# Twelve units on half the tokens first, none of them stored, and the products of chunks 2 and 3 stepped between those of chunks 0 and 1

## The chip, the cores and the metric

The kernel runs on one core of a Trainium2 chip. The metric is the device time of the whole program in microseconds (us), from the first to the last instruction with what lies around them. Three runs of the kernel before gave a median of 1481.88 us.

## The reference

Three stages follow each other. `S` is 768 steps, `N` is 4 x 768 = 3072 tokens.

```
for t in range(S):                       # 4 batches, 8 heads, 48 x 48 state
    S_re, S_im = ar*S_re - ai*S_im + k v^T, ar*S_im + ai*S_re
    y[:, :, t] = q . S_re
x = y as (3072, 384)
out = sum over 4 experts of p_e * (relu(x @ w1[e]) @ w2[e])   # 1024 wide each
h = out @ w_in                           # 2048 wide
result = maximum(0.01*h, h) @ w_out
```

`a` is first scaled so that its magnitude is at most 0.999, and `p` is the expert probability divided by its sum.

## The kernel before

**Tiling.** The recurrence is cut into 24 chunks of 128 steps. For a chunk, `elementwise(c)` (17 steps, on VectorE, ScalarE and GpSimd) makes decayed and rotated queries and keys in the tile `ft`, and six DMAs (`by_head`, L251) rearrange it by head into `hd`. `products(c)` (9 steps) is TensorE work: transposes `pt` copied to `kt`, scores `sc` masked into `att`, the state update `pm` into `st`, the output `py` copied to `y`, and transposes `px` split into `xh` and `xl`, a high and a low part whose sum is the fp32 value. Four chunks fill a token group of 512.

**Units.** The first weight stage is 32 units of 128 hidden columns, the second 16. A unit of the first stage is loaded as `raw` (384 KB, L392), split into two parts by `split_unit` (ScalarE cast L408, GpSimd difference L409; once for the in-weights, part 0, and once for the out-weights, part 1), and used: `gemm_in` (L455) makes `ph`, VectorE and ScalarE turn it into `hp` (L460), `hh` (L472) and `hl` (L473), and `gemm_out` (L484 to L486) adds into three accumulators. Six parts are split early instead, with TensorE making the difference (`cast_early` L419, `rest_early` L429 to L431). A unit that was split is stored to `ws_scratch` (768 KB, L626), and later groups load it from there (L400).

**Order.** The program is recorded by hand, and each engine runs its instructions in the order of recording. `PLAN` is the order of the start: digits step `elementwise`, `p` and `q` step the products of chunks 0 and 1, `s` and `m` are `cast_early` and `rest_early`. The list `order` then names the units. In group 0, eight units run on tokens 0 to 255 (chunks 0 and 1), then the same eight on tokens 256 to 511 (chunks 2 and 3), and units 8 to 31 on all 512. For each entry, `gemm_in` stands two entries ahead of `gemm_out`, and between the halves of an entry `tick` takes up to three steps of `background()`: the rest of chunks 2 and 3, their products (`r`, `t`), and all later chunks at a pace set by a table. SyncE issues nearly all DMAs, in order, so a DMA that waits for its data holds up those behind it.

**Names.** "In block" and "out block" are the nine matmuls of one `gemm_in` or `gemm_out`; "in 5" is that of the entry 5. "Pair" is the two wide matmuls of one `rest_early`.

Of the kernel before, what the change touches and what calls it, by code (L numbers as in the profile page):

```python
# [19 lines left out]
P = 128  # L20
# [12 lines left out]
AR_MIN = 0.76  # L33
NHALF = 8
PLAN = (
    "0101001010101011" "01ss0000mm" "00sss11mm000" "1111ppsm23111qq"
    "23232n3pp23p2ppqq3q23qqpq23m"
)
MAXT = 3
KN = 3.0  # L40
PT = 32
TPOOL = 6
MARGIN = 2.0
LAG = 2
E2 = 20
RAWS = 4
# [5 lines left out]
NSTEPS = ESTEPS + len(PSTEPS)  # L52
WAIT = 4
AR_MAX = 1e4
# [7 lines left out]
def fused_kernel(  # L62
# [20 lines left out]
    with ExitStack() as fast:  # L83
# [58 lines left out]
        def load_chunk(c, part=None):  # L142
            if part in (None, 0):
                pool = p_el2 if c in (1, 3) else p_in
                t = pool.tile([P, 4, NG, P], F32, name="aaqk", bufs=2)
                vt = pool.tile([P, DM], F32, name="vt", bufs=2 if c in (1, 3) else 3)
                inputs[c] = (t, vt)
            t, vt = inputs[c]
            if part is None:
                SP.dma_start(t, attn[c])  # L150
            else:
                SP.dma_start(t[:, 2 * part : 2 * part + 2], attn[c][:, 2 * part : 2 * part + 2])
            if part in (None, 1):
                SP.dma_start(vt, v[c])
# [3 lines left out]
        def table(name):  # L158
            if tables[0] != name:
                A.preload_act_table_set(name)  # L160
                tables[0] = name

        def elementwise(c):
# [79 lines left out]
        def by_head(c):  # L243
# [4 lines left out]
            for ri in range(2):  # L248
                for i in range(NG):
                    row = ri * D + i * DG  # L250
                    (A if c < 2 and (i == ri or i == 2 - ri) else SP).dma_start(hd[row : row + DG], ft[:, ri, i])  # L251
            feats[c] = (ft, hd, vt)
# [5 lines left out]
        def products(c):  # L258
# [7 lines left out]
            for ri in range(2):  # L266
                pt = ps_a.tile([P, NG, P], F32, name="pt", tag="pa")
                for i in range(NG):
                    PE.transpose(pt[:, i], ft[:, ri, i, P : 2 * P], ident)  # L269
                A.copy(  # L270
                    kt[:, :, ri * D : (ri + 1) * D].rearrange("t h (r d) -> t r d h", d=DG),
# [28 lines left out]
            for h in range(H):  # L300
                PE.matmul(py[:, h], att[:, h], vt[:, h * D : (h + 1) * D], start=True, stop=first)  # L301
                if not first:
                    PE.matmul(py[:, h], hd[:, h, :P], old[:, h], start=False, stop=True)  # L303
                if h == 3:
                    yield
# [62 lines left out]
        second_stage = lambda g: [(g, u, whole) for u in range(NU1, NU)]  # L368
        order = [(0, u, half) for half in halves for u in range(NHALF)] + first_stage(0)[NHALF:]
        begins = [0]  # L370
# [10 lines left out]
        raws, wts, pbs, hs, x2 = {}, {}, {}, {}, {}  # L381
        seen = set()
        fresh = [u not in seen and not seen.add(u) and u < NU1 for _, u, _ in order]

# [51 lines left out]
        def load_pb(s):  # L436
            if s >= len(order) or order[s][1] >= NU1 or order[s][1] % 8 or order[s][2][0]:
                return
            g, e = order[s][0], order[s][1] // 8
            pb = p_h.tile([P, TG], F32, name="pb", bufs=2)  # L440
            SP.dma_start(pb, pn_d[e : e + 1, g * TG : (g + 1) * TG].to_broadcast([P, TG]))
# [34 lines left out]
        def gemm_out(s, acc):  # L476
            u, (t0, t1) = order[s][1:]
            first, last = u in (0, NU1) and t0 == 0, u in ends
            wt = wts.pop(s)[:, 1]
            hh, hl = hs.pop(s)  # L480
            for dc in range(NG):
                cols = slice(dc * P, (dc + 1) * P)
                out = acc[dc][:, t0:t1]
                PE.matmul(out, wt[:, 0, cols], hh, start=first, stop=False)  # L484
                PE.matmul(out, wt[:, 1, cols], hh, start=False, stop=False)  # L485
                PE.matmul(out, wt[:, 0, cols], hl, start=False, stop=last)  # L486


        def zipped(*gens):
            gens = list(gens)  # L490
            while gens:
                for x in list(gens):
                    if next(x, gens) is gens:
                        gens.remove(x)
                yield

        def run_all(*gens):
            gens = list(gens)
            while gens:
                gens = [x for x in gens if next(x, gens) is not gens]  # L500

        with tc.manual_schedule():
# [12 lines left out]
            steps.update(zip("pqrt", (products(c) for c in range(CPG))))  # L515
            early_halves = iter([(s, part) for s in range(6) for part in (0, 1)][: PLAN.count("s")])
            for x in PLAN + "m" * 8:
                if x in steps:
# [6 lines left out]
                elif x == "m":  # L525
                    rest_early()
            for s in (5, 6):
                load_unit(s)
            split_unit(3, 0)

            def background():
                for _ in range(2):
                    next(steps["2"])
                    yield
                for _ in zipped(steps["2"], steps["3"]):
                    yield
# [36 lines left out]

            first = 2 + max(0, ESTEPS + 1 - min(PLAN.count("2"), PLAN.count("3"))) + WAIT + E2 - PLAN.count("r") - PLAN.count("t")
            pace = [(0.0, 0), (KN, first)]
# [33 lines left out]
            for s in range(len(order)):  # L609
# [14 lines left out]
                split_h(s + 2, hp)  # L624
                if fresh[s]:
                    SP.dma_start(ws[u], wts[s].bitcast(F32))  # L626
# [216 lines left out]
```

## Time and profile before

| | us |
|---|---|
| median of three runs | 1481.88 |
| lowest, highest | 1481.4, 1482.5 |
| the profiled execution | 1478.36 |
| its span, first to last instruction | 1476.6 |
| TensorE busy (95% of the span) | 1402.4 |
| VectorE busy (59%) | 864.7 |
| ScalarE busy (38%) | 564.8 |
| GpSimd busy (18%) | 264.5 |

The page cuts the span into 40 slices of 37 us and gives each engine's busy share in tenths; a 9 is 90% or more. An engine whose row is all nines has no room there. The view of waits says for whom an engine stood idle, the timeline gives each instruction its start and duration, and the view by windows gives busy time and granted TensorE clock of any stretch. A clock of 1.00 is 2.4 GHz, 0.50 is 1.2 GHz.

### The profile page before, as it was taken

What the parts mean: (1) busy time and instruction counts of PE and PEld (TensorE: products, weight loads), DVE (VectorE), ACT (ScalarE), POOL (GpSimd) and SP (SyncE); (2) the same over time, 40 slices, a digit from 0 to 9 for tenths busy, and PEclk for the clock granted to TensorE, in tenths of its full rate; (3) what the DMA queues carried; (4) which work ended last, traced back from release to release, by engine and by line L of the source; (5) the groups of instructions that cost most, each with busy time, mean ns of one, the idle gap of its engine ahead of it and who ended that gap; (6) DMA issues with size and microseconds to landing.
All of it is one profiled execution on the core that took longest, in us unless ns stands there. A gap on an engine that the chain in (4) does not pass through costs nothing.

```text
span 1476.6 us, 18540 instructions
## 1 busy us (share of the span) xinstructions
PE 1402.4 (95%) x6978; PEld 1177.2 (80%) x6978; DVE 864.7 (59%) x1504; ACT 564.8 (38%) x961; POOL 264.5 (18%) x244
## 2 busy tenths in 40 slices
PE   3858999999999999999999999999999999999997
PEld 1858888888777888788888888888888888888886
DVE  7556887788988898785454554554443333333332
ACT  5424565444345434455234354233332111323232
POOL 2120565412223223221011110110110000100000
PEclk9569999999999999999999999999999999999999
DMA  7288789986788789588567477576465665556561
GB/s 192 43 207 301 212 255 298 331 291 208 273 301 290 250 305 319 153 303 245 153 234 222 151 242 216 188 222 199 154 199 172 231 207 196 190 188 208 190 212 65
DMA packets 91043, 325.49 MB, mean 220 GB/s; under 512 B 10464, under 2 KB 32064, under 8 KB 90944
## 3 DMA queue, kind: packets, MB, share of 16 engines
q1 hardware_dynamic: 87488, 318.71, 67.1%
q10 hardware_dynamic: 3456, 5.51, 1.3%
q8 instruction: 56, 0.92, 0.3%
q14 instruction: 43, 0.35, 0.1%
HBM read 262.72 MB, written 42.52 MB: 207 GB/s over the span
## 4 chain that ended last, share of the span: by engine, by line
PE 58%; DVE 2%; ACT 0%; issue 0%; DVEq 0%; ACTq 0%
PE ph L455 27%; PE acc L484 9%; PE acc L486 9%; PE acc L485 9%; PE sc L280 1%; PE py L301 1%; PE py L303 1%; PE pm L289 1%; PE pt L269 0%; DVE hl L473 0%; DVE hp L460 0%; PE px L311 0%; DVE d L349 0%; ACT hh L472 0%; DVE d L355 0%
## 5 line engine op out<-in xcount | busy, mean ns | idle before, releaser
L455 PE MATMUL ph<-xh,wt 128*128 128x512 f32 (+1 forms) x1200 | 397.9, 388 | 0.0
L484 PE MATMUL acc<-hh,wt 128*128 128x512 f32 (+1 forms) x888 | 350.8, 395 | 5.2 <-ACT o L604 5.1
L486 PE MATMUL acc<-hl,wt 128*128 128x512 f32 (+1 forms) x888 | 342.9, 386 | 4.5 <-DVE hl L473 4.5
L485 PE MATMUL acc<-hh,wt 128*128 128x512 f32 (+1 forms) x888 | 341.5, 385 | 0.0
L472 ACT CAST hh<-hp 128x512 fp32r<-128x512 f32 (+1 forms) x296 | 180.4, 610 | 418.2 <-DVE hp L460 326.5
L473 DVE TENSOR_TENSOR hl<-hp,hh 128x512 fp32r<-128x512 f32 (+1 forms) x296 | 213.4, 721 | 150.3 <-ACT hh L472 149.1
L455 PEld LDWEIGHTS ph<-xh,wt 128*128 128x128 f32 x1200 | 225.5, 190 | 42.4 <-ACT ge L121 0.3
L460 DVE SCALAR_TENSOR_TENSOR hp<-ph,pb 128x512 f32<-128x512 f32 (+1 forms) x200 | 133.0, 665 | 189.9 <-PE ph L455 188.6
L455 PE MATMUL ph<-xl,wt 128*128 128x512 f32 (+1 forms) x600 | 230.2, 384 | 0.0
L486 PEld LDWEIGHTS acc<-hl,wt 128*128 128x128 f32 x888 | 167.3, 188 | 40.0 <-DVE hl L473 6.0
L455 PE MATMUL ph<-x2h,wt 128*128 128x512 f32 x576 | 198.3, 398 | 0.0
L484 PEld LDWEIGHTS acc<-hh,wt 128*128 128x128 f32 x888 | 167.7, 189 | 36.5 <-ACT o L604 5.8
L485 PEld LDWEIGHTS acc<-hh,wt 128*128 128x128 f32 x888 | 168.0, 189 | 30.7
L463 DVE SCALAR_TENSOR_TENSOR hp<-hp 128x512 f32<-128x512 f32 x96 | 72.0, 750 | 185.0 <-ACT hp L462 184.9
L455 PEld LDWEIGHTS ph<-xl,wt 128*128 128x128 f32 x600 | 114.1, 190 | 20.3 <-DVE xl L320 0.2
L455 PEld LDWEIGHTS ph<-x2h,wt 128*128 128x128 f32 x576 | 108.7, 189 | 25.1
L462 ACT COPY hp<-ph 128x512 f32<-128x512 f32 x96 | 56.3, 586 | 178.5 <-PE ph L455 178.5
L455 PE MATMUL ph<-x2l,wt 128*128 128x512 f32 x288 | 114.5, 397 | 0.0
L409 POOL TENSOR_TENSOR wt<-raw,wt 128x384 fp32r<-128x384 f32 x58 | 65.0, 1142 | 62.4 <-ACT wt L408 62.3
L643 POOL TENSOR_TENSOR x2l<-o,x2h 128x512 fp32r<-128x512 f32 x18 | 25.2, 1424 | 256.4 <-ACT x2h L642 256.4
L301 PE MATMUL py<-vt,att 128*128 128x48 f32 x384 | 70.9, 280 | 0.1
L280 PEld LDWEIGHTS sc<-hd 96*128 96x128 f32 x384 | 54.2, 208 | 15.4 <-issue 7.9
(97 smaller groups left out, 1482.2 us busy)
## 6 DMA issues: line engine op xcount, KB each, us to landing
wt<-ws_scratch SPq DMA_DIRECT2D x264, 768.0 KB, 4.8
ws_scratch<-wt SPq DMA_DIRECT2D x32, 768.0 KB, 7.5
hd<-ft SPq DMA_DIRECT2D x138, 128.5 KB, 5.4
aaqk<-in_attn_dram SPq DMA_DIRECT2D x22, 768.0 KB, 8.9
raw<-in_w_dram SPq DMA_DIRECT2D x32, 384.0 KB, 4.5
r<-in_w_dram SPq DMA_DIRECT2D x32, 384.0 KB, 7.4
ws_scratch<-dw SPq DMA_DIRECT2D x32, 384.0 KB, 6.2
pb<-pn_scratch SPq DMA_DIRECT2D x24, 256.0 KB, 6.5
```

What stands on the lines that cost most here:

```text
L280: PE.matmul(sc[:, j], hd[:, h, P : 2 * P], hd[:, h, :P], start=True, stop=True)
L301: PE.matmul(py[:, h], att[:, h], vt[:, h * D : (h + 1) * D], start=True, stop=first)
L409: G.tensor_tensor(wt[:, 1], raw, wt[:, 0].bitcast(F32), ALU.subtract)
L455: PE.matmul(ph[:, : t1 - t0], wt[:, wi, cols], x[kc][:, t0:t1], start=n == 0, stop=n == 3 * NG - 1)
L460: V.scalar_tensor_tensor(hp, ph, 0.0, pbs[g, u // 8][:, t0:t1], ALU.max, ALU.mult)
L462: A.copy(hp, ph)
L463: V.scalar_tensor_tensor(hp, hp, 0.01, hp, ALU.mult, ALU.max)
L472: A.copy(hh, hp)
L473: V.tensor_tensor(hl, hp, hh.bitcast(F32), ALU.subtract)
L484: PE.matmul(out, wt[:, 0, cols], hh, start=first, stop=False)
L485: PE.matmul(out, wt[:, 1, cols], hh, start=False, stop=False)
L486: PE.matmul(out, wt[:, 0, cols], hl, start=False, stop=last)
```

## The change

The list `order` runs twelve units on tokens 0 to 255, then units 12 to 19 on all 512, and then alternates: the second half of unit 0, unit 20 whole, the second half of unit 1, unit 21 whole, and so on to unit 31. The first halves store nothing; the twelve second halves load `raw` again, split it again and store it, so the eight loads from `ws_scratch` in group 0 are gone and twelve loads of `raw` are new. Twelve parts instead of six are split early on TensorE. `PLAN` is rewritten, the products of chunk 1 get four additional 384-column matmuls (`warm`) whose result nobody reads, their `kt` copies go from ScalarE to VectorE, and three `hd` DMAs of chunk 1 go from ScalarE's queue to SyncE's. `LATER` orders the rest of the elementwise steps of chunks 2 and 3.

```
-NHALF = 8
+NHALF = 12
 PLAN = (
-    "0101001010101011" "01ss0000mm" "00sss11mm000" "1111ppsm23111qq"
-    "23232n3pp23p2ppqq3q23qqpq23m"
+    "0101001010101011" "01ss0000mm" "00sss11mm000" "1111ppsmsm23111L"
+    "23n22qqsmsm33ppsm22p3ppmsqqm3qsm2233qqpqm"
 )
+LATER = "23222232232223333333"
-KN = 3.0
+KN = 5.0
-WAIT = 4
+WAIT = 22
...
+        def warm(n):
+            out = ps_acc.tile([P, TG], F32, name="warm", tag="acc0")
+            for _ in range(n):
+                PE.matmul(
+                    out[:, : NG * P], ident, inputs[0][0][:, 0].rearrange("p g t -> p (g t)"),
+                    start=True, stop=True,
+                )
...
-                    (A if c < 2 and (i == ri or i == 2 - ri) else SP).dma_start(hd[row : row + DG], ft[:, ri, i])
+                    (A if c == 0 and (i == ri or i == 2 - ri) else SP).dma_start(hd[row : row + DG], ft[:, ri, i])
...
-                A.copy(
+                (V.tensor_copy if c == 1 else A.copy)(
...
+                if c == 1 and h % 2:
+                    warm(1)
...
-        order = [(0, u, half) for half in halves for u in range(NHALF)] + first_stage(0)[NHALF:]
+        order = [(0, u, halves[0]) for u in range(NHALF)] + first_stage(0)[NHALF : NU1 - NHALF]
+        for u in range(NHALF):
+            order += [(0, u, halves[1]), (0, NU1 - NHALF + u, whole)]
...
-        fresh = [u not in seen and not seen.add(u) and u < NU1 for _, u, _ in order]
+        fresh = [g == 0 and u < NU1 for g, u, _ in order]
...
+            parts = [(t0, t1)]
+            if (order[s][0], u) == (0, NHALF):
+                parts = list(halves)
...
             def background():
-                for _ in range(2):
-                    next(steps["2"])
-                    yield
-                for _ in zipped(steps["2"], steps["3"]):
+                for x in LATER:
+                    next(steps[x], None)
                     yield
...
-                if fresh[s]:
+                if fresh[s] and t1 == TG:
                     SP.dma_start(ws[u], wts[s].bitcast(F32))
```

What moves is shown at three places. The first is TensorE between the output of chunk 0 (`py`, L301, now L311) and the end of the products of chunk 1. Before:

```order
L301 MATMUL py<-vt,att 128x48 x8
L280 MATMUL sc<-hd 128x128 x8
L289 MATMUL pm<-vt,kt 96x48 x8
L301 MATMUL py<-vt,att 128x48
L303 MATMUL py<-st,hd 128x48
```

Now:

```order
L311 MATMUL py<-vt,att 128x48 x8
L442 MATMUL ph<-raw,ident 128x384
L443 MATMUL ph<-wt,minus 128x384
L290 MATMUL sc<-hd 128x128 x8
L442 MATMUL ph<-raw,ident 128x384
L443 MATMUL ph<-wt,minus 128x384
L299 MATMUL pm<-vt,kt 96x48 x8
L442 MATMUL ph<-raw,ident 128x384
L443 MATMUL ph<-wt,minus 128x384
L311 MATMUL py<-vt,att 128x48
L313 MATMUL py<-st,hd 128x48
```

Pairs of wide matmuls now stand between the narrow ones.

The second place is ScalarE around the copies `kt` of chunk 2 (`kt_657` before, `kt_833` now), with buffer numbers; `raw_509` and `raw_718` are each the newest unit whose part 0 is cast there (unit 7 before, unit 11 now). Before:

```order
L408 CAST wt_567<-raw_467 128x384
L472 CAST hh_643<-hp_637 128x256
L270 COPY kt_657<-pt_658 128x48x8
L270 COPY kt_657<-pt_663 128x48x8
L408 CAST wt_670<-raw_509 128x384
```

Now:

```order
L488 CAST hh_801<-hp_799 128x256
L421 CAST wt_816<-raw_718 128x384
L421 CAST wt_784<-raw_674 128x384
L280 COPY kt_833<-pt_834 128x48x8
L280 COPY kt_833<-pt_839 128x48x8
```

The cast of the newest unit moved from behind the two copies to ahead of them.

The third place is SyncE's queue from the `hd` pieces of chunk 2 on; `aaqk` and `vt` are the inputs of chunk 4. Before:

```order
L626 DMA ws_scratch<-wt 128x1536 x2
L251 DMA hd<-ft 16x8x257 x12
L150 DMA aaqk<-in_attn_dram 128x1536
L154 DMA vt<-in_v_dram 128x384
L626 DMA ws_scratch<-wt 128x1536
```

Now:

```order
L457 DMA pb_628<-pn_scratch 128x512
L261 DMA hd<-ft 16x8x257 x6
L405 DMA raw<-in_w_dram 128x768
L261 DMA hd<-ft 16x8x257 x6
L151 DMA aaqk<-in_attn_dram 128x1536
L155 DMA vt<-in_v_dram 128x384
L405 DMA raw<-in_w_dram 128x768 x7
```

The `raw` of unit 10 stands between the `hd` pieces of chunks 2 and 3, and those of units 11 to 17 behind chunk 3's and the inputs of chunk 4.

## Rows read from the trace of the kernel before

**Rows 1.** The page: its first line, and TensorE's busy tenths in 40 slices.

```profile
span 1476.6 us, 18540 instructions
...
PE   3858999999999999999999999999999999999997
```

**Rows 2.** Windows: stretch, length, busy time (instructions) by engine, clock, DMA share, GB/s.

```profile
36.00:66.00 30.00, 25.32 (x120) 24.19 (x121) 13.38 (x31) 11.04 (x21) 0.00 (x0) 0.50 0.25 43
...
123.00:170.00 47.00, 41.44 (x271) 37.07 (x269) 37.63 (x73) 27.56 (x51) 17.59 (x16) 0.96 0.71 213
...
222.00:259.00 37.00, 35.77 (x192) 29.90 (x191) 28.91 (x47) 22.07 (x39) 21.87 (x20) 1.00 0.95 302
259.00:296.00 37.00, 37.00 (x206) 31.68 (x206) 26.79 (x40) 18.29 (x33) 15.40 (x14) 1.00 0.97 331
```

**Rows 3.** TensorE's waits, 66 to 128 us: in total, times, longest.

```profile
PE pt L269 <- DVE ft L234: 9.4, 1, 9.4
PE sc L280 <- DMA hd<-ft: 5.4, 1, 5.4
```

**Rows 4.** TensorE's timeline, products of chunks 0 and 1: start, duration, what [idle before].

```profile
36.47 3.79 PE L280 MATMUL sc<-hd 96*128 96x128 f32 x16 [2.04 <-ACT kt L270]
...
44.47 2.79 PE L289 MATMUL pm<-vt,kt 128*96 128x48 f32 x16 [4.21 <-DVE att L281]
47.06 3.61 PE L301 MATMUL py<-vt,att 128*128 128x48 f32 x16
...
63.33 1.67 PE L311 MATMUL px<-ident,y 128*128 128x128 f32 x6
...
66.74 0.58 PE L455 MATMUL ph<-xh,wt 128*128 128x256 f32 x1
```

**Rows 5.** Windows: one microsecond after `py` of chunk 2 (columns as above).

```profile
107.00:108.00 1.00, 0.68 (x7) 0.55 (x5) 0.00 (x0) 0.29 (x1) 0.00 (x0) 0.82 1.04 430
```

**Rows 6.** TensorE's timeline at the full clock: a pair, an out block's start, products.

```profile
24.97 0.81 PE L429 MATMUL ph<-raw,ident 128*128 128x384 f32 x2
25.62 0.81 PE L430 MATMUL ph<-wt,minus 128*128 128x384 f32 x2
...
70.27 0.28 PE L484 MATMUL acc<-hh,wt 128*128 128x256 f32 x1
...
71.35 0.28 PE L455 MATMUL ph<-xh,wt 128*128 128x256 f32 x1
...
112.35 1.16 PE L280 MATMUL sc<-hd 96*128 96x128 f32 x8 [0.56 <-ACT kt L270]
...
115.32 1.48 PE L289 MATMUL pm<-vt,kt 128*96 128x48 f32 x16
...
122.01 0.55 PE L311 MATMUL px<-ident,y 128*128 128x128 f32 x3 [0.57 <-ACT y L307]
```

**Rows 7.** The chain that ended last: a whole unit's in block.

```profile
623.15 2.10 PE ph L455 x9
```

**Rows 8.** VectorE's timeline: chunk 2's wait at 39 us, `ft` of chunks 2 and 3.

```profile
39.03 0.56 DVE L185 TENSOR_TENSOR ta<-ta,tb 128x384 f32<-128x384 f32 x1 [5.33 <-ACT ta L121]
...
85.77 0.95 DVE L234 TENSOR_TENSOR ft<-cs,aaqk 128x768 f32<-128x768 f32 x1
...
87.78 2.62 DVE L234 TENSOR_TENSOR ft<-cs,aaqk 128x768 f32<-128x768 f32 x2
```

**Rows 9.** ScalarE's timeline: the table load ahead of chunk 2's elementwise work.

```profile
37.08 1.28 ACT L160 ACT_TABLE_LOAD   x1
```

**Rows 10.** SyncE's timeline: the `hd` pieces of chunks 2 and 3.

```profile
86.75 7.71 SPq L251 DMA_DIRECT2D hd<-ft  x12
```

**Rows 11.** Windows: transfers while `hd` pieces move, and while units' loads and stores do.

```profile
96.00:100.00 4.00, 4.00 (x22) 4.00 (x21) 1.20 (x2) 0.00 (x0) 0.00 (x0) 0.50 1.18 122
...
172.00:174.00 2.00, 2.00 (x12) 1.65 (x10) 1.97 (x5) 0.00 (x0) 0.00 (x0) 1.00 1.02 415
```

**Rows 12.** Groups by line, GpSimd, 150 to 262 us: count | busy, mean ns | idle before.

```profile
L409 POOL TENSOR_TENSOR wt<-raw,wt 128x384 fp32r<-128x384 f32 x43 | 48.8, 1158 | 26.0 <-ACT wt L408 25.9
```

More of the change, by code (lines that the diff above doesn't have):

```diff
@@ L44 @@
 LAG = 2
-E2 = 20
+E2 = 17
 RAWS = 4
@@ L145, in load_chunk @@
                 t = pool.tile([P, 4, NG, P], F32, name="aaqk", bufs=2)
-                vt = pool.tile([P, DM], F32, name="vt", bufs=2 if c in (1, 3) else 3)
+                vt = (p_el2 if c == 1 else p_in).tile([P, DM], F32, name="vt", bufs=1 if c == 1 else 3)
                 inputs[c] = (t, vt)
@@ L381, in fused_kernel @@
         raws, wts, pbs, hs, x2 = {}, {}, {}, {}, {}
-        seen = set()
-        fresh = [u not in seen and not seen.add(u) and u < NU1 for _, u, _ in order]
+        fresh = [g == 0 and u < NU1 for g, u, _ in order]
         def load_unit(s):
@@ L439, in load_pb @@
             g, e = order[s][0], order[s][1] // 8
-            pb = p_h.tile([P, TG], F32, name="pb", bufs=2)
+            if g == 0 and e * 8 < NHALF:
+                pb = pools["raw"].tile([P, TG], F32, name=f"pb{e}")
+            else:
+                pb = p_h.tile([P, TG], F32, name="pb", bufs=2)
             SP.dma_start(pb, pn_d[e : e + 1, g * TG : (g + 1) * TG].to_broadcast([P, TG]))
@@ L480, in gemm_out @@
             hh, hl = hs.pop(s)
+            parts = [(t0, t1)]
+            if (order[s][0], u) == (0, NHALF):
+                parts = list(halves)
             for dc in range(NG):
                 cols = slice(dc * P, (dc + 1) * P)
[L483 to L494, printed above, removed]
-                yield
[L497 to L500, printed above, removed]
+                for a0, a1 in parts:
+                    out = acc[dc][:, a0:a1]
+                    hhp, hlp = hh[:, a0 - t0 : a1 - t0], hl[:, a0 - t0 : a1 - t0]
+                    PE.matmul(out, wt[:, 0, cols], hhp, start=first, stop=False)
+                    PE.matmul(out, wt[:, 1, cols], hhp, start=False, stop=False)
+                    PE.matmul(out, wt[:, 0, cols], hlp, start=False, stop=last)
         with tc.manual_schedule():
@@ L515, in fused_kernel @@
             steps.update(zip("pqrt", (products(c) for c in range(CPG))))
-            early_halves = iter([(s, part) for s in range(6) for part in (0, 1)][: PLAN.count("s")])
-            for x in PLAN + "m" * 8:
+            early_halves = iter([(s, part) for s in range(7) for part in (0, 1)][: PLAN.count("s")])
+            for x in PLAN:
                 if x in steps:
@@ L526, in fused_kernel @@
                     rest_early()
-            for s in (5, 6):
-                load_unit(s)
-            split_unit(3, 0)
+                elif x == "L":
+                    load_unit(5)
+                    load_unit(6)
             def background():
-                for _ in range(2):
-                    next(steps["2"])
-                    yield
-                for _ in zipped(steps["2"], steps["3"]):
+                for x in LATER:
+                    next(steps[x], None)
                     yield
@@ L572, in fused_kernel @@
             dec = decoding()
-            first = 2 + max(0, ESTEPS + 1 - min(PLAN.count("2"), PLAN.count("3"))) + WAIT + E2 - PLAN.count("r") - PLAN.count("t")
+            first = len(LATER) + WAIT + E2
             pace = [(0.0, 0), (KN, first)]
```

## The prediction

> **What bounds the kernel now.** I read the slices of the page first: TensorE is at 90% or more from the fifth slice to the end [rows 1], so from about 150 us on the time is TensorE's own work, and only the first 150 us hold room. Then I read the waits and the windows of that part. Between 36 and 66 us TensorE is busy 25.3 of 30 us, but at a clock of 0.50 [rows 2]: the products of chunks 0 and 1 run at half speed. The first in block starts at 66.74 [rows 4]; I call that moment T0. After T0 TensorE stands 9.4 us for `ft` of chunk 2 and 5.4 us for its `hd` [rows 3]. The transposes `px` of chunk 3 end at 122.01 + 0.55 = 122.56 [rows 6], 55.8 us after T0. From 123 to 170 us only 47.0 - 41.4 = 5.6 us are idle [rows 2], and less later. So the change can gain in three ways: an earlier T0, more gemm work done before 122.56, and fewer waits after it.
>
> **The start, up to T0.** Six more pairs stand on TensorE, and four `warm` matmuls. At full clock a matmul of 384 columns takes 25.62 - 24.97 = 0.65 us [rows 6], a pair 1.3 us. The products at half clock and at full clock, from rows: a block of 8 `sc` 3.79 against about 2.1 us (half of it 1.16 with its tail), `pm` 2.79 against 1.48 [rows 4, 6], `py` of chunk 0 3.61 us [rows 4] against an estimated 1.8, `py` of chunk 1 twice that.
>
> What releases them moves too. The table load at 37.08 [rows 9] comes earlier, because ScalarE no longer issues three DMAs of chunk 1 nor copies its `kt`; two casts and a difference copy take some of that room. I put it at 33.5, and VectorE's wait of 5.33 us at 39.03 [rows 8] shrinks by 3.6 us. VectorE's `kt` copies then end at about 38.4, so `sc` of chunk 0 starts at about 38.6 instead of 36.47 [rows 4]; it has two more pairs ahead of it in any case. From there TensorE has no long wait that I can find, and I add at full clock: `sc` 2.1, pair 1.3, `pm` 1.5, `py` 1.8, pair 1.3, `sc` 2.1, pair 1.3, `pm` 1.5, pair 1.3, `py` 3.6 with four `warm` 2.6, which is 20.4 us, to 59.0. Of what follows, `px`, `xh` and `xl`, about 1.8 us are uncovered: T0 at 60.8, **5.9 us earlier**.
>
> The clock is the choice in this. Before, narrow matmuls alone did not raise it in 30 us, and behind `py` of chunk 2 it fell again at 107 (0.82 on the way to 0.50 [rows 5]); at 115.32 `pm` still ran fast behind `sc` [rows 6]. With pairs between the narrow blocks I take the full clock, since the row at 115 is the nearer one. If it falls for the second half, `sc`, `pm` and `py` of chunk 1 cost 1.7 + 1.3 + 3.3 = 6.3 us more.
>
> The Trainium skill, "TensorE: Matmul & The Clock Gate", section "Why this matters for your kernels", asks only that TensorE be kept busy without a pause to reach its high clock. By that page alone the pairs and `warm` would buy no clock and just cost their 6 x 1.3 + 2.6 = 10.4 us, against 3.6 from the earlier table load: T0 at 73.5, and the sum +7.4 instead of the -5.3 below. The 25.3 busy microseconds at 0.50 [rows 2] contradict it, so it gets no chance here.
>
> **T0 to the end of the products of chunk 3.** VectorE paces this. Before, `ft` of chunk 2 was ready at 85.77 + 0.95 = 86.72 and that of chunk 3 at 90.40 [rows 8]: 20.0 and 23.7 us after T0. In the new order six scans (2.7 us) are done ahead of T0, about two more `hp` and `hl` (1.8 us) stand between, and `ft` of chunk 2 goes ahead of the last steps of chunk 3. I get 17.5 and 23.5 us after T0. While VectorE works, TensorE gets through ten in and seven out blocks instead of five and three.
>
> Then comes what I think is the new bound. Twelve `hd` pieces took 7.7 us to issue [rows 10] and moved at 122 GB/s [rows 11]; six of them are 0.79 MB, 6.4 us. So chunk 3's move from 25.3 to 31.7 us after T0. Behind them on SyncE's queue stand the inputs of chunk 4 (0.98 MB) and `raw` of unit 11 (0.39 MB), at 415 GB/s [rows 11] another 3.3 us: it lands at about 36 us after T0. ScalarE casts unit 11 ahead of the `kt` copies of chunk 2, and `sc` needs the buffer that `kt` frees. So `sc` of chunk 2 starts at about 37.8 instead of 95.70 - 66.74 = 29.0 (its wait ended there). TensorE stands for about 9 us, and the clock falls. From there to the end of `px` of chunk 3 I count five blocks and two chunks' products, 20.9 us at full clock, 2.4 for the clock, 2.1 for the known short waits: 25.4. The stretch is 63.2 us instead of 55.8: **7.4 us longer**.
>
> In return more is done by then. Before, eight in and six out blocks had run; now it is twelve and ten. A half block is 71.35 - 70.27 = 1.08 us [rows 6], so 8 x 1.08 = **8.6 us less remain**.
>
> **What is added after.** Four more units are cut in two: each costs 4 x 1.08 - 2 x 2.10 [rows 7] = 0.12 us, and unit 12's out block is cut as well: 0.6, with the spread of these blocks **0.8 us**. In 12 now stands right behind `px` of chunk 3 and waits for `xh` and `xl`; before, an out block stood between: **1.0 us**. The other waits of 123 to 170 us I leave as large as they are: some of them came from halves that are gone, and GpSimd gets new work. That work is 18 more differences at 1.158 us [rows 12], 21 us, and ScalarE as many casts; GpSimd is busy 21.9 of 37 us there [rows 2], and at this load they hide. Were GpSimd full, they would cost up to 21 us.
>
> **Sum:** -5.9 + 7.4 - 8.6 + 0.8 + 1.0 = **-5.3 us**. The profiled execution took 1478.36 us, its span 1476.6, and the median is 1481.88. I put the difference on the median: **1476.6 us**. A difference below 0.2%, 3.0 us, can't be told from none.
>
> **The rivals.**
>
> *Transfers too slow in the alternation (slower).* A second half and a whole unit, 2.16 + 4.20 = 6.4 us of TensorE, now move two stores of 0.79 MB and two loads of 0.39 MB: 2.36 MB. Twelve such and three chunks at 1.77 MB are 33.6 MB against 76 + 3 x 8.6 = 102 us of TensorE. Needed are 330 GB/s. Before, 331 were sustained over 37 us at a share of 0.97 without a wait, but only 302 in the stretch ahead [rows 2]. At 302 it takes 111 us: 9 us more, 1485.6. It decides from below 330 GB/s on; four buffers of `raw` hold a load at most three entries ahead, so a late one stops ScalarE and then TensorE. Against it: single stretches reach 415 [rows 11], and with `hd` at its own pace I get 19 + 31.2 MB / 415 = 94 us.
>
> *The limit of the HBM.* If the weights moved at a steady 358 GB/s and `hd` as above, the transfers would take 19 + 87 = 106 us, 4 us over TensorE's 102: 1480.6. The Trainium skill, "DMA: Bandwidth & Descriptors", section "Where 436 GB/s comes from", states 358 as the limit of one core's share of the HBM. By that rule this change would be bound by it; the window at 415 speaks against it.
>
> *The clock falls in the products of chunk 1.* T0 at 67.1: -5.3 + 6.3 = +1.0, 1482.9. For it speaks the fall at 107, against it the row at 115.
>
> *Unit 11 lands early, or its cast doesn't block.* Then `sc` of chunk 2 starts when its `hd` lands and TensorE gets there, about 29 us after T0: 8.8 us less, 1467.8. For it: several DMAs are in flight at once, so `raw` may pass. Against it: the 122 GB/s lasted as long as `hd` moved, with a load of inputs already issued behind it.
>
> **How the numbers follow.** The forecast (1473 to 1479) gets 0.50, slow transfers 0.17, the limit of the HBM 0.05, the fallen clock 0.15, the early unit 11 0.13. Faster: 0.44 of the forecast, the early unit 0.13, and the lower edges of the limit and the clock 0.05, together 0.62. Same: 0.05 of the forecast, 0.08 of the clock, 0.02 of the limit, 0.03 of the slow transfers, 0.18. Slower: the other 0.20. The range goes from 1467 to 1486; both ends take in the rivals up to their own prices and leave about 2 in 10 outside.
>
> **What would show it.** Right: the first in block near 61 us; a clock of 1.00 from 37 us to it; `sc` of chunk 2 waiting some 9 us, with ScalarE waiting for `raw` of a weight cast just ahead of `kt`; `px` of chunk 3 ending near 124; TensorE without long waits after. Wrong: half clock in `py` of chunk 1; `sc` of chunk 2 released by `hd` instead; TensorE waiting for GpSimd or for weights between 160 and 270 us, with the transfers at a share near 1.

## The result, and the profile after

The changed kernel took **1496.3 us** (median of 4 runs, 1495.9 to 1498.7) against 1481.6 us (4 runs, 1480.8 to 1482.5): a ratio of 1.0107, 95% interval 1.0090 to 1.0124. It is slower by 14.7 us. The prediction was 1476.6 us with a range of 1467 to 1486, so sign and range are both wrong. The profiled execution of the changed kernel took 1495.9 us, close to its median; that of the kernel before took 1478.4, 3.2 us below its median. Some 3 us of any difference between these two traces are spread of the runs. Their spans differ by 17.6 us: 13.2 arise up to the emptying of the accumulators of group 0 (at 285.7 us before, at 298.9 now), and 4.4 behind it, where no cause was looked for. One of the twelve executions of the experiment e7 below took 2295.5 us at a granted clock of 0.58; without it the median of e7 is 1479.2 us instead of 1479.4.

The first line of the page and TensorE's busy tenths in 40 slices of 37 us, to be read against [rows 1]:

```profile
span 1494.2 us, 18843 instructions
...
PE   4869898899999999899999999999999999999997
```

The fifth to the eighth slice, 149 to 299 us, were all 9 before and are 9, 8, 8, 9 now. The windows of the changed kernel (stretch, length, busy time by engine, granted clock, DMA share, GB/s) cut the time at the first in block, at the end of the products of chunk 3, and where the accumulators of group 0 are emptied (299 us, before 286):

```profile
36.00:59.00 23.00, 21.85 (x144) 17.29 (x143) 15.32 (x31) 12.60 (x27) 2.08 (x2) 1.00 0.62 137
60.00:124.00 64.00, 47.88 (x344) 45.24 (x344) 33.25 (x61) 19.82 (x42) 18.47 (x17) 0.85 0.37 84
124.00:299.00 175.00, 152.38 (x884) 132.70 (x884) 133.51 (x211) 95.67 (x177) 95.69 (x84) 0.94 0.85 266
```

The same last stretch of the kernel before:

```profile
123.00:286.00 163.00, 155.12 (x884) 133.32 (x883) 129.24 (x214) 92.64 (x167) 80.54 (x72) 0.99 0.86 266
```

This pair of rows holds the result. Before, TensorE was idle for 163.0 - 155.1 = 7.9 us of that stretch, and the clock cost another 1.7 (in windows of half a microsecond, busy time times what the clock lacks to 1.00, added up). Now it is idle for 175.0 - 152.4 = 22.6 us, and the clock costs 8.0. That is 14.7 + 6.3 = 21 us more lost. The stretch should have become 7 us shorter and became 12 us longer; the work in it fell by the other 9. TensorE's waits there (in total, times, longest):

```profile
PE sc L290 <- DMA hd<-ft: 13.4, 4, 4.3
PE pt L279 <- DVE ft L244: 5.6, 1, 5.6
PE px L323 <- ACT y L319: 2.7, 2, 1.8
```

Each of chunks 4 to 7 waits at `sc` for its `hd`, and chunk 4 for its `ft`. Behind the longer stops the clock is low. The last `sc` stop, and the five microseconds that follow:

```profile
269.70 3.76 PE L290 MATMUL sc<-hd 96*128 96x128 f32 x16 [4.13 <-DMA hd<-ft]
```

```profile
270.00:275.00 5.00, 5.00 (x25) 5.00 (x25) 3.05 (x5) 1.78 (x4) 2.19 (x3) 0.50 1.01 419
```

So a stop of 4.1 us costs about 2.5 us more at half clock (5.0 x 0.50).

### The profile page after: what moved, and what is told of

Its sections match the earlier page's. It is cut to its first block, busy times and chain, and to the rows that moved or that the text cites. A ratio compares the mean times of both kernels' runs of the same rounds, so it can differ in the third digit from the quotient of the medians.

```text
span 1494.2 us, 18843 instructions
## 1 busy us (share of the span) xinstructions
PE 1410.0 (94%) x7091; PEld 1180.6 (79%) x7091; DVE 879.9 (59%) x1514; ACT 577.2 (39%) x993; POOL 289.3 (19%) x262
## 4 chain that ended last, share of the span: by engine, by line
PE 57%; issue 0%; ACT 0%; DVE 0%
PE ph L471 26%; PE acc L505 9%; PE acc L507 9%; PE acc L506 9%; PE sc L290 1%; PE py L311 1%; PE py L313 1%; PE pm L299 1%; PE pt L279 0%; PE px L323 0%; DVE hp L479 0%; ACT o L610 0%; ACT hh L488 0%; ACT hp L478 0%; ACT dw L369 0%
## 5 line engine op out<-in xcount | busy, mean ns | idle before, releaser
L505 PE MATMUL acc<-hh,wt 128*128 128x512 f32 (+1 forms) x903 | 354.2, 392 | 8.3 <-ACT o L610 5.0
L507 PE MATMUL acc<-hl,wt 128*128 128x512 f32 (+1 forms) x903 | 346.8, 384 | 1.4 <-DVE hl L489 1.3
L506 PE MATMUL acc<-hh,wt 128*128 128x512 f32 (+1 forms) x903 | 346.2, 383 | 0.0
L489 DVE TENSOR_TENSOR hl<-hp,hh 128x512 fp32r<-128x512 f32 (+1 forms) x300 | 219.9, 733 | 156.9 <-ACT hh L488 154.6
L471 PEld LDWEIGHTS ph<-xh,wt 128*128 128x128 f32 x1224 | 229.7, 191 | 44.9 <-ACT xh L331 1.8
L505 PEld LDWEIGHTS acc<-hh,wt 128*128 128x128 f32 x903 | 172.1, 191 | 39.9 <-ACT o L610 5.4
L507 PEld LDWEIGHTS acc<-hl,wt 128*128 128x128 f32 x903 | 172.0, 190 | 36.1 <-DVE hl L489 2.7
L506 PEld LDWEIGHTS acc<-hh,wt 128*128 128x128 f32 x903 | 172.5, 191 | 30.9
L422 POOL TENSOR_TENSOR wt<-raw,wt 128x384 fp32r<-128x384 f32 x76 | 87.2, 1169 | 72.8 <-ACT wt L421 68.3
L290 PE MATMUL sc<-hd 96*128 96x128 f32 x384 | 54.3, 289 | 23.1 <-DMA hd<-ft 13.4
```

The costliest lines, as they stand in the source:

```text
L290: PE.matmul(sc[:, j], hd[:, h, P : 2 * P], hd[:, h, :P], start=True, stop=True)
L422: G.tensor_tensor(wt[:, 1], raw, wt[:, 0].bitcast(F32), ALU.subtract)
L471: PE.matmul(ph[:, : t1 - t0], wt[:, wi, cols], x[kc][:, t0:t1], start=n == 0, stop=n == 3 * NG - 1)
L489: V.tensor_tensor(hl, hp, hh.bitcast(F32), ALU.subtract)
L505: PE.matmul(out, wt[:, 0, cols], hhp, start=first, stop=False)
L506: PE.matmul(out, wt[:, 1, cols], hhp, start=False, stop=False)
```

## What was predicted until 124 us held

TensorE's timeline of the changed kernel: the first in block, `sc` of chunk 2, `px` of chunk 3 and the first in block of a whole unit.

```profile
60.37 0.38 PE L471 MATMUL ph<-xh,wt 128*128 128x256 f32 x1 [0.62 <-ACT xh L331]
...
98.76 2.07 PE L290 MATMUL sc<-hd 96*128 96x128 f32 x8 [9.68 <-ACT kt L280]
...
123.28 0.84 PE L323 MATMUL px<-ident,y 128*128 128x128 f32 x3
124.69 0.55 PE L471 MATMUL ph<-xh,wt 128*128 128x512 f32 x1 [0.57 <-ACT xh L331]
```

The first in block was predicted at 60.8 us and came at 60.37, with the clock at 1.00 from 36 to 59 us (first window above; before 0.50, [rows 2]). `sc` of chunk 2 was to start 37.8 us after it, with a stop of about 9: it started after 38.4, with one of 9.68. The cause was right too. ScalarE waits for the raw weights of unit 11 just ahead of `kt`, and they land 36.7 us after the first in block, predicted 36 (its own terms, 31.7 and 3.3, add to 35.0):

```profile
97.07 0.93 ACT L421 CAST wt<-raw 128x384 fp32r<-128x384 f32 x2 [7.94 <-DMA raw<-in_w_dram]
97.90 1.47 ACT L280 COPY kt<-pt 128x384 f32<-128x384 f32 x2
```

`px` of chunk 3 ended 63.75 us after the first in block, predicted 63.2. So the start and the stretch are met within 1 us. Some of that is luck: `sc` of chunk 0 started at 39.48 us, 0.9 later than predicted, and what stands between it and the first in block took 1.3 less than predicted; and from `sc` of chunk 2 to the end of `px` of chunk 3 the prediction has 2.4 us for the clock and 2.1 for short waits, the trace 4.1 and 0.6. Of the work moved ahead, the trace shows the twelve in and ten out blocks that were predicted. Of the kernel before it shows eight in and five out blocks by 122.56, not six (the sixth had just begun), so 9 x 1.08 = 9.7 us less remained instead of 8.6. What turned the sum round lies behind 124 us.

## Experiments

The table gives the medians; the ratio is to the kernel before, whose median was 1481.3 to 1481.9 us in every group of runs. Unless said otherwise an experiment is the changed kernel with the one edit shown.

| run | us | ratio (95%) |
|---|---|---|
| changed kernel | 1496.3 | 1.0107 (1.0090 to 1.0124) |
| e1 stores with the first halves | 1497.8 | 1.0112 (1.0095 to 1.0130) |
| e2 cast of unit 11 behind `kt` | 1496.4 | 1.0100 (1.0082 to 1.0119) |
| e3 `sc` three steps later | 1500.9 | 1.0139 (1.0120 to 1.0158) |
| e4 raw loads issued later | 1491.6 | 1.0071 (1.0056 to 1.0086) |
| e5 chunk 4 begun earlier | 1488.1 | 1.0046 (1.0032 to 1.0061) |
| e6 = e4 + e5 | 1482.6 | 1.0017 (1.0007 to 1.0027) |
| e7 = e1 + second halves reload the split | 1479.4 | 0.9987 (0.9977 to 0.9998) |
| e8 new start, order of before | 1475.1 | 0.9962 (0.9948 to 0.9976) |
| e9 = e1, low parts read back | 1490.6 | 1.0059 (1.0042 to 1.0076) |
| e10 = e1, high parts read back | 1544.5 | 1.0430 (1.0412 to 1.0449) |
| e11 = e8 without `warm` | 1468.2 | 0.9917 (0.9899 to 0.9935) |
| e12 = e7 + e4 + e5 | 1477.2 | 0.9971 (0.9962 to 0.9981) |
| e13 = e1, casts only | 1487.6 | 1.0047 (1.0031 to 1.0063) |
| e14 = e1, differences only | 1493.6 | 1.0083 (1.0066 to 1.0100) |
| e15 = e11 + e4 | 1468.4 | 0.9921 (0.9902 to 0.9940) |

Three theories came out of the trace. T: the transfers of the alternation hold `hd` up. P: the steps of a chunk are placed too close behind one another. S: the issue of `hd` stands on SyncE behind a load of raw weights, which waits until GpSimd has freed a buffer. S has a row ahead of the runs. SyncE's timeline, and VectorE's `ft` of chunk 7, done at 253.76 + 1.31 = 255.07:

```profile
257.05 0.33 SPq L405 DMA_DIRECT2D raw<-in_w_dram  x1
257.43 0.45 SPq L632 DMA_DIRECT2D ws_scratch<-wt  x1
257.98 4.95 SPq L261 DMA_DIRECT2D hd<-ft  x6
```

```profile
253.76 1.31 DVE L244 TENSOR_TENSOR ft<-cs,aaqk 128x768 f32<-128x768 f32 x1
```

`hd` goes out 2.9 us after its data are there. Over chunks 4 to 7 it is 8.5 us in all, before the change 3.0.

**e1, the stores.**

```diff
-                if fresh[s] and t1 == TG:
+                if fresh[s] and t0 == 0:
```

> The twelve cut units store their split weights with the first half instead of the second, so a pair of the alternation moves one store and two loads, 1.57 MB instead of 2.36 MB. Theory T (the transfers of the alternation hold `hd` up): the four waits of `sc` for `hd`, 13.4 us, fall below 4 us, and the time goes from 1496.3 to about 1482. Theory P (the steps of a chunk are placed too close behind one another: TensorE comes to `sc` 8.3 to 10.5 us after `ft` is done, before the change 10.5 to 12.4): these waits stay between 10 and 15 us, the time between 1493 and 1498. Theory S (the issue of `hd` stands on SyncE behind a load that waits for GpSimd): as P.

A third of the bytes of a pair are gone, and the time is 1497.8 us. In its profiled execution, which at 1504.2 us was longer than the rest of its runs, 9.4 us are waited for `hd` instead of 13.4, with the DMA share at 0.74 between 124 and 286 us. But the total hides what the stores cost where they went. A cast on ScalarE now waits for a buffer of `wt` that a store still reads, just ahead of `kt`, and `sc` of chunk 2 stands 14.12 us instead of 9.68. ScalarE's row of e1, then TensorE's:

```profile
103.92 0.92 ACT L421 CAST wt<-raw 128x384 fp32r<-128x384 f32 x2 [1.53 <-DMA ws_scratch<-wt]
```

```profile
105.60 2.08 PE L290 MATMUL sc<-hd 96*128 96x128 f32 x8 [14.12 <-ACT kt L280]
```

`px` of chunk 3 ends 69.8 us after the first in block, 6.1 more than in the changed kernel, and the whole is only 1.5 longer. So an estimated 4 to 5 us were gained behind it. T is not worth the 14 us that it was priced at, but a part of that size is not refuted. The runs built on e1 (e7, e9, e10, e12 to e14) all have this longer stretch (69.6 to 70.8 us), so comparing them with e1 is fair.

**e2, the cast of unit 11.** At the entry s == 7 the two casts stand behind the chunk's steps:

```diff
-                split_unit(s + 4, 0)
-                split_unit(s + 3, 1)
+                late = s == 7
+                if not late:
+                    split_unit(s + 4, 0)
+                    split_unit(s + 3, 1)
...
                     tick(now)
+                if late:
+                    split_unit(s + 4, 0)
+                    split_unit(s + 3, 1)
```

> ScalarE casts unit 11 behind the two `kt` copies of chunk 2 instead of ahead of them; nothing else moves. If the stall of 9.7 us at `sc` of chunk 2 comes from that cast, as the prediction said, the wait falls below 1.5 us, `px` of chunk 3 ends about 8.8 us earlier after the first in block (near 54 us instead of 63), and the time goes from 1496.3 to about 1487.5. Rival: the stall only moves (to the in block of unit 11, which needs that cast, or to `ft` of chunk 4, which waits for its inputs): less than 3 us gained, 1493 to 1497.

The rival is right: 1496.4 us, no change. The stop at `sc` is gone (0.8 us left), but the cast, still waiting for the weights until 96.95, now holds the `hh` that VectorE's `hl` and then `att` need. TensorE's timeline of this run:

```profile
89.87 1.16 PE L290 MATMUL sc<-hd 96*128 96x128 f32 x8 [0.85 <-ACT kt L280]
...
99.47 0.66 PE L311 MATMUL py<-vt,att 128*128 128x48 f32 x2 [5.16 <-DVE att L291]
...
123.56 0.71 PE L323 MATMUL px<-ident,y 128*128 128x128 f32 x3
```

`px` of chunk 3 comes at 123.56 instead of 123.28. So the late transfer holds whatever stands behind that cast on ScalarE; an order with the cast still further back was not tried.

**e3, `sc` later.** For chunks 4 to 7:

```diff
+PSTEPS1 = (1, 3, 5, 15, 17, 19, 21, 23, 25)
...
+                    psteps = PSTEPS1 if c < 2 * CPG else PSTEPS
...
-                        next(todo if k in PSTEPS else ahead, None)
+                        next(todo if k in psteps else ahead, None)
```

> For chunks 4 to 7 the `sc` blocks come three steps later behind the issue of `hd`, `pm` two and `py` one; the number of steps is the same. Theory P: a step is 0.2 units, three are 2.5 us, so the waits of `sc` fall from 13.4 us to about 4, the clock falls less often after them (about 1 us each), and the time goes to about 1484 (1482 to 1487). The wait of 5.6 us for `ft` of chunk 4 stays. Theory T: `hd` lands as late as before and TensorE waits for it the less; the same here, so this run measures what the waits are worth. Rival: products that stand closer behind `sc` wait for `att` and `y` instead, 1 to 2 us each chunk: 1490 to 1494.

1500.9 us, worse than all that was expected. The waits for `hd` fall to 1.5 us, and others take their place:

```profile
PE pm L300 <- DVE att L292: 7.7, 3, 4.5
PE pt L280 <- DVE ft L245: 5.6, 1, 5.6
PE py L312 <- DVE att L292: 2.6, 1, 2.6
```

The stall that was moved by re-spacing came back one step on. What is looked for is a cause that makes the chain of a chunk longer, and P in this form is not it.

**e4, the raw loads later.** The call goes from the head of an entry to its end:

```diff
-                load_unit(s + 7)
                 load_split(s + 5)
...
                         next(dec, None)
+                load_unit(s + 7)
```

> The load of raw weights is issued at the end of an entry of the order instead of its start, so SyncE waits for GpSimd behind the chunk's steps and not ahead of them. Theory S: `hd` of chunks 4 to 7, issued 1.3 to 2.9 us after `ft` was done (8.5 us in all), goes out within 0.3 us of it; the waits of `sc` fall from 13.4 us to about 6, the time from 1496.3 to about 1488. Theory T: `hd` lands as late as before, waits 12 to 15 us, 1494 to 1498. Theory P alone: the waits stay above 9 us.

1491.6 us, 4.7 gained of the 8 expected. `hd` of chunks 4 to 7 now goes out within 0.12 us of `ft`, and no wait for it is left, but 4.9 us for `att` are new:

```profile
PE pt L279 <- DVE ft L244: 5.6, 1, 5.6
PE py L311 <- DVE att L291: 4.9, 2, 2.6
PE px L323 <- ACT y L319: 2.8, 2, 2.0
```

S is a part, and about 5 us of the loss.

**e5 and e6, chunk 4 begun earlier.** Eight of its steps run beside the products of chunk 3, and the pace counts eight steps less:

```diff
-                for x in "rt":
-                    yield from steps[x]
+                yield from steps["r"]
+                el = elementwise(CPG)
+                for _ in steps["t"]:
+                    next(el)
+                    yield
...
-                for _ in elementwise(CPG):
+                for _ in el:
...
-first + ESTEPS + (NSTEPS + 1)
+first + ESTEPS - 8 + (NSTEPS + 1)
```

> Eight of the 17 elementwise steps of chunk 4 run beside the products of chunk 3 instead of behind them, where VectorE is idle; that also leaves 117 steps instead of 125 for the 25 units after, 4.68 a unit instead of 5. Theory P (too little TensorE work between the steps of a chunk): the wait for `ft` of chunk 4 falls from 5.6 us to 2 or less, its 2 us at half clock behind it go as well, and the waits for `hd` fall from 13.4 to about 8, since a chunk gets 1.6 us more cover: 1496.3 - 3.6 - 2 - 5 - 2 = about 1484 (1482 to 1489). Rival, from the run before in which a stall only moved: what is gained at `ft` is waited for at `hd`, `att` and `y`, and the time stays within 3 us, 1493 to 1498.

> The early steps of chunk 4 and the later issue of the raw loads together. If the two causes (too little cover, SyncE held by a load ahead of `hd`) are separate, the gains add up: 4.7 us of the one, as measured, and 8 to 12 of the other, 1480 to 1484. If both stand for the same waits, the time is that of the better one alone, 1484 to 1491.

e5 gave 8.3 us of the 12 expected. e6 gave 13.7, about the sum of 8.3 and 4.7: the two gains add up. Room between the steps does matter where VectorE is idle beforehand. But both only give the chain of a chunk more time, and neither says why it needs more than before.

**e7, the stored split read back.** On e1:

```diff
-        fresh = [g == 0 and u < NU1 for g, u, _ in order]
+        seen = set()
+        fresh = [u not in seen and not seen.add(u) and u < NU1 for _, u, _ in order]
```

> The second halves read the split weights that the first halves stored, as before the change, in the new order: 24 casts on ScalarE and 24 differences on GpSimd leave the alternation, and a pair moves 1.97 MB (1.57 where only the stores moved, 2.36 in the changed kernel). Theory G (the added casts and differences hold VectorE's steps up: single steps of chunk 4 took 1.4 and 3.0 us where they took 0.6 and 1.9 before): against the run in which only the stores moved, 1497.8, at least 6 us are gained, 1486 to 1492. Without G: within 3 us of it, 1495 to 1501.

1479.4 us: 18.4 less than e1 and 16.9 less than the changed kernel, with the order and the pace of the changed kernel. It is the largest single step of all these runs, and beyond the range of theory G. TensorE's waits from the end of the products of chunk 3 to the emptying of group 0, and 50 us of the alternation:

```profile
PE pt L279 <- DVE ft L244: 5.4, 1, 5.4
PE px L323 <- ACT y L319: 0.6, 1, 0.6
PE ph L472 <- ACT xh L331: 0.6, 1, 0.6
```

```profile
200.00:250.00 50.00, 49.41 (x323) 44.17 (x322) 41.08 (x73) 25.87 (x49) 24.55 (x21) 1.00 0.88 320
```

No wait for `hd` is left, at 320 GB/s, more than the changed kernel's 302 in the same window. A pair moves more here than in e1, and the steps are as far apart, so neither is the larger part of the loss. What is gone is 24 casts and 24 differences, and with them the twelve loads of `raw` whose buffers they hold. The chain of a chunk shows it: from `ft` of chunk 4 to `ft` of chunk 8 (ends) it is 291.57 - 151.90 = 139.7 us in the changed kernel, 130.9 before, and 279.01 - 161.10 = 117.9 here. VectorE's rows of the changed kernel, then of e7:

```profile
149.29 2.61 DVE L244 TENSOR_TENSOR ft<-cs,aaqk 128x768 f32<-128x768 f32 x2
...
290.62 0.95 DVE L244 TENSOR_TENSOR ft<-cs,aaqk 128x768 f32<-128x768 f32 x1
```

```profile
158.48 2.62 DVE L244 TENSOR_TENSOR ft<-cs,aaqk 128x768 f32<-128x768 f32 x2
...
278.06 0.95 DVE L244 TENSOR_TENSOR ft<-cs,aaqk 128x768 f32<-128x768 f32 x1
```

**e9 and e10, one kind of work each, the other half read back.** On e1, the low (e9) or the high (e10) parts of a second half are loaded from the store:

```diff
+        def load_part(s, i):
+            if s < len(order) and fresh[s] and order[s][2][0]:
+                wts[s] = p_w.tile([P, 2, 2, DM], F32R, name="wt", bufs=WTS)
+                SP.dma_start(wts[s][:, :, i].bitcast(F32), ws[order[s][1]][:, :, i])
...
-            G.tensor_tensor(wt[:, 1], raw, ...)
+            if not order[s][2][0]:
+                G.tensor_tensor(wt[:, 1], raw, ...)
...
+                load_part(s + 4, 1)
```

(e10: the same with `load_part(s + 4, 0)` and the condition on the cast.)

> Stores with the first halves as in the run that moved only them (1497.8), the second halves still load raw weights and ScalarE still casts them, but the low parts of the split are read back (0.39 MB) instead of computed: 24 differences leave GpSimd, 24 casts stay on ScalarE. The run without casts and differences gave 1479.4. Theory G (GpSimd's differences: they hold the raw buffers and with them SyncE's queue, and they stretch VectorE's instructions that run at the same time): most of the 18.5 us are gained, 1479 to 1485. Theory A (ScalarE's casts stand ahead of the steps of the chunks): little is gained, 1492 to 1498.

> The mirror of the run without differences: the high parts are read back, so 24 casts leave ScalarE, and GpSimd still makes the 24 differences from raw weights. Theory G: 1492 to 1498. Theory A: 1479 to 1485. If both share the loss evenly, both runs lie near 1488.

Both were spoilt by waits that the edit brought. In e9 (1490.6, 7.2 less than e1) TensorE waits 5.7 us for the parts read back, so what the missing differences bring by themselves can't be read from it. In e10 (1544.5, far outside both ranges) differences wait for their transfers and hold their raw buffers for that time. GpSimd's and SyncE's waits there, 131 to 349 us:

```profile
POOL wt L429 <- DMA wt<-ws_scratch: 58.6, 8, 11.6
```

```profile
SPq L405 <- POOL wt L429: 142.3, 24, 10.1
```

e10 says nothing about casts, but it shows the links of the chain: a late difference holds a raw buffer, and the buffer holds SyncE's queue. The 47 us above e1 are not the price of that chain alone: TensorE itself waits 18.6 us there for parts read back, and for `hd` 11.4 us, against 9.4 in e1.

**e13 and e14, the cleaner pair.** On e1, nothing is read back. TensorE multiplies with the part that is made, in place of both:

```diff
-                G.tensor_tensor(wt[:, 1], raw, ...)      (e13, second halves only)
...
-                A.copy(wt[:, 0], raw)                    (e14, second halves only)
```

> On the run in which only the stores moved (1497.8): the second halves load raw weights and ScalarE casts them, but GpSimd makes no difference for them and nothing is read back; TensorE takes the high parts in place of the low ones, so that part of the computation is left out (as many matmuls, other numbers). Unlike the run that read the low parts back, no new transfer can be waited for. Theory G: 1478 to 1485. Theory A: 1493 to 1498. Shared evenly: about 1489.

> The mirror: the second halves load raw weights, GpSimd makes the 24 differences (raw minus raw), ScalarE casts nothing for them, and TensorE takes the differences in place of the high parts; that part of the computation is left out. Theory G: 1493 to 1498. Theory A: 1478 to 1485. The run that read the high parts back took 1544, since a difference there had to wait for a transfer and held its raw buffer for that time; if that chain was the reason, this run without it is far below 1544.

Without the differences 1487.6 us, 10.2 less than e1; without the casts 1493.6, 4.2 less; without either (and without their raw loads, e7) 18.4 less. e14 lies in the range of theory G, e13 in neither and near an even share. So GpSimd's differences are the larger part and ScalarE's casts the smaller; the other 4 us go when both do, or with the raw loads, which no run takes away alone. The pair is not free of side effects: in e14 a difference no longer waits for its cast, and in e13 the cast alone sets a raw buffer free. The waits of e13 and of e14 up to the emptying of group 0:

```profile
PE pt L279 <- DVE ft L244: 5.6, 1, 5.6
PE sc L290 <- DMA hd<-ft: 4.8, 2, 4.4
PE px L323 <- ACT y L319: 1.3, 2, 1.0
```

```profile
PE sc L290 <- DMA hd<-ft: 7.6, 3, 3.9
PE pt L279 <- DVE ft L244: 5.5, 1, 5.5
PE px L323 <- ACT y L319: 1.7, 2, 1.5
```

**e8 and e11, the start alone.** The changed kernel with the order, the eight halves, the reload and the pace of before; e11 leaves `warm` out:

```diff
-NHALF = 12
+NHALF = 8
-KN = 5.0
+KN = 3.0
-WAIT = 22
+WAIT = 0
...
-                if c == 1 and h % 2:
-                    warm(1)
```

(The last two lines are e11's.)

> The new start alone: the order of the entries, eight units in halves, the reload of second halves and the pace over 27 units are those of before; the new sequence of steps up to the first in block, the pairs, the `warm` matmuls, and chunk 1's `hd` and `kt` off ScalarE are kept. The first in block comes at about 60.5 instead of 66.74. If the 5.9 us stay gained, the time is 1481.6 - 5.9 = 1475.7 (1474 to 1478). Rival: `ft` of chunks 2 and 3 depends on VectorE, which comes no earlier by as much, so TensorE just waits longer at chunk 2's transposes: 1480 to 1482.

> The new start alone (1475.1) without the four wide `warm` matmuls in `py` of chunk 1. If they are what keeps the clock up there, `py`, `px` and the first in blocks run at half clock: 1.7 to 6 us lost against 2.6 us of `warm` saved, so 1474 to 1479 with a granted clock near 0.5 before the first in block. If the pairs are enough, the clock stays at 1.00 and 2.6 us are gained at the first in block; VectorE's `ft` of chunk 2 then takes them back, 1473 to 1475.5.

e8 took 1475.1 us, expected 1475.7: the 5.9 us that the prediction gave to the start stay gained (this start also takes six casts and six differences from ScalarE and GpSimd, 52 instead of 58). e11 took 1468.2, 13.2 us less than before, 7 less than e8 and less than either range expected. The clock did not need `warm` in `py`. The windows of e11 up to `px` of chunk 1 and behind it:

```profile
36.00:57.00 21.00, 18.61 (x136) 15.69 (x136) 15.14 (x31) 12.40 (x27) 2.09 (x2) 1.00 0.70 174
57.00:60.00 3.00, 2.69 (x12) 2.50 (x13) 0.86 (x2) 0.05 (x1) 0.00 (x0) 0.64 0.00 0
```

The sixteen narrow matmuls of `py` run at 1.00, and the clock falls for some 4 us only afterwards. The first in block comes at 57.1 instead of 60.3. That explains 3 of the 7 us; e8's profiled execution was the fastest of its six (1469.4), so the trace can't show the rest, and it stays open.

**e12 and e15, put together.** The edits are those of e7, e4 and e5, and of e11 and e4.

> Second halves read the stored split (1479.4 by itself), eight steps of chunk 4 beside the products of chunk 3, raw loads issued later. The wait of 5.4 us for `ft` of chunk 4 that was left goes, with 2 us of half clock behind it; the later raw loads bring nothing here, since `hd` went out within 0.1 us of `ft` without them. 1479.4 - 6 = about 1473 (1471 to 1476). Rival: the early steps cost what they gain, 1478 to 1481.

> The new start alone, without `warm` (1468.15), with the raw loads issued at the end of an entry. `hd` of some chunks goes out 1.3 to 1.6 us after `ft` there, and 3.0 us of waiting for `hd` are left: at most 3 us gained, 1465 to 1468.5; as in the changed kernel, a wait that goes may come back at `att` or `y`, then no difference.

e12 gained 2.2 us on e7, not 6: the wait for `ft` of chunk 4 fell to 1.9 us, but 1.7 us at `sc` and 1.7 for a cast are new. In e15 the later issue brings nothing (1468.4 and 1468.2), as expected where the added splits are missing. e11 and e15, which can't be told apart, are the fastest kernels of the study.

## Why the prediction was wrong

- **The step that failed** is "GpSimd is busy 21.9 of 37 us there, and at this load they hide". The prediction had counted the work rightly (18 more casts and differences; the traces have 76 against 58) and named the price itself, up to 21 us. Taking 24 of each away, with their raw loads, brought 18.4 us (e1 to e7): 10.2 with the differences alone (e13), 4.2 with the casts alone (e14). The 1479.4 us of e7 are 3 us from the forecast, though it also bears the 6 us of e1's early stores. A share of 0.6 did not mean room, and the loss did not show where the prediction looked for it: TensorE waited for `hd` and `ft`, hardly for GpSimd or weights. The differences were in three chains at once. They free the raw buffers, on which SyncE waited 97.2 us between 124 and 299 against 64.6 before (123 to 286), with `hd` behind it; e4 prices this at 4.7 us. They run in line with GpSimd's own steps of a chunk (at 193.03 one starts right where a pair of differences ends); no run prices that. And VectorE's instructions take longer beside them: the three scans of `th` of chunk 4 took 1.87 us before, with a multiplication on GpSimd beside part of them, and 3.04 now. VectorE's row and GpSimd's at the same time, in the changed kernel:

```profile
142.88 3.04 DVE L226 TENSOR_TENSOR_SCAN th<-ones,th,tr 128x128 f32<-128x128 f32 x3
```

```profile
143.42 2.22 POOL L422 TENSOR_TENSOR wt<-raw,wt 128x384 fp32r<-128x384 f32 x2
```

  Over 124 to 286 us the scan of `tb` takes 844 ns a piece in the changed kernel, 603 before, and 658 and 650 in e13 and e7, which have no added differences (726 in e14, which has them). That the stretching costs the time that e4 leaves is argued from these durations; no run isolates it. The Trainium skill, "Trainium Architecture — The Big Picture", section "What this means for kernel authors", says that VectorE and GpSimd share a pair of ports to SBUF under an exclusive lock; the rows agree in that the instructions take longer side by side, and do not show a lock.
- "The other waits of 123 to 170 us I leave as large as they are" fell with it. Only the work that came was weighed, by its engine's load and not by what queues behind it. Before, the second halves needed no split: GpSimd made no difference between 111.2 and 142.6 us, while chunk 4 was prepared. Now it makes four pairs between 125.1 and 145.6 us.
- The stop for `ft` of chunk 4 was not looked for: its elementwise steps begin behind the first whole `hp`, at 128.0, and need 23.9 us, where TensorE has 22.4 us of work from `px` of chunk 3 on. The stop is there without the added splits too (5.4 us in e7). e5 prices it, with the wider pace, at 8.3 us.
- **Of the rivals**, slow transfers had the right sign (1485.6, chance 0.17) by a mechanism that e7 refutes for the larger part of the loss; of e1's 4 to 5 us a part may be its. The limit of the HBM has a figure against it again: e6 moves 364 GB/s from 250 to 300 us, above the 358 that the Trainium skill, "DMA: Bandwidth & Descriptors", section "Where 436 GB/s comes from", states as the limit. Unit 11 landing early did not happen. That its cast doesn't block was forced in e2 and brought nothing: the price of 8.8 us was not reached, since ScalarE held the next thing instead.
- **The clock.** It rose as predicted, but `warm` was judged wrongly: e11's narrow `py` runs at 1.00 without it, and the fall behind it, some 1.6 us by its windows, costs less than the four wide matmuls, 4 x 0.71 us. The clock also fell without a pause. The changed kernel has these windows at the end of `py` of chunk 3 and behind it, with TensorE busy all the time:

```profile
118.00:120.00 2.00, 2.00 (x21) 2.00 (x20) 1.06 (x2) 0.00 (x0) 0.00 (x0) 1.00 0.45 166
120.00:122.00 2.00, 2.00 (x17) 2.00 (x17) 0.00 (x0) 0.48 (x2) 0.00 (x0) 0.86 0.01 4
122.00:124.00 2.00, 2.00 (x10) 1.72 (x9) 0.42 (x1) 0.30 (x2) 0.00 (x0) 0.50 0.00 0
```

  So the trace disagrees here with the Trainium skill, "TensorE: Matmul & The Clock Gate", section "Why this matters for your kernels", which asks only for no pause; the chance of nothing that the prediction gave to that page was right. What in these narrow products lets the clock fall, no run here shows.
- **Terms that were right**: the start (-5.9; e8 -6.2), the stretch to `px` of chunk 3 (+7.4; 63.75 instead of 55.8 is +7.9), and the wait behind it (1.0; 0.57). The work moved ahead (-8.6) is -9.7 by the blocks counted above; what cutting the blocks costs (0.8) no run shows by itself.

## What to carry to other kernels

Work added to an engine that is 60% busy hides only if nothing that the bound engine waits for stands behind it: follow what the new instruction frees (a buffer, a queue), what shares its engine, and what slows down beside it. A stall that is only re-spaced or re-ordered came back one wait later here (e2, e3); what helps is to take work out of the chain (e7) or to start the chain earlier in an idle stretch (e5). Look at where an edit moves work to as well as where it takes it from: e1's total hid an estimated gain of 4 to 5 us behind a loss of 6 elsewhere. Test the parts of a change one by one: here the start alone, without its extra matmuls, is 0.8% faster than before, and the rest of the change hides that.

## What was not expected of the hardware

TensorE's stops cost more than themselves. The stops of 3.4 to 5.6 us in the stretch from 124 to 299 us were each followed by 3 to 5 us at a lower clock (0.50 from 270 to 275 above), those of 1.6 and 1.8 us were not, and in e2 the clock stayed at 0.50 from 98 to 112 us behind one of 5.2. VectorE's three scans of `tb` of chunk 4 took 1.06 us before, with GpSimd idle, and 1.75 in the changed kernel, where a pair of differences ran beside part of them; GpSimd's pairs of differences took from 1.97 to 3.42 us there.
